# The second tile's first slices on other PSUM banks, five of them begun early, and the last batch's v in the buffer of the q and k rows

## The chip, the cores and the metric

The kernel runs on one core of one Trainium2 chip, in one launch. The metric is the device time of an execution in microseconds (us); the median of three runs is given. Engines are called as in the profile: PE (TensorE, matrix products), DVE (VectorE), ACT (ScalarE), POOL (GpSimd, which here also issues most loads) and SP (SyncE, which issues transposing DMAs and stores). PSUM has eight banks; each holds one 128 x 512 result in f32.

## The reference, cut to what matters

```python
def _attn_ref(q, k, v):                    # q, k, v: (8, 8, 576, 64) f32
    scores = scale * np.matmul(q, k.transpose(0, 1, 3, 2))
    rel = pos[:, None] - pos[None, :]
    mask = (rel >= 0) & (rel < 64)         # each row sees itself and the 63 rows before it
    ...                                    # softmax over the masked scores
    return np.matmul(attn, v)

def _moe_ref(x, w_in, w_out):              # x: (4608, 512), w_in: (512, 2048), w_out: (2048, 512)
    h = x @ w_in
    g = h * np.cos(h)
    return g @ w_out
```

The output of the attention, with the heads side by side, is x of the second part: 8 batches x 576 rows = 4608 rows of 512.

## The kernel before

**The tiles.** The 4608 rows are nine tiles (mt 0 to 8) of 512 rows. For a tile PE makes 16 slices of h (`first`, L347): slice ff is a 128 x 512 result summed over four k-steps `ks`, one for each pair of heads. ACT takes sin(h + pi/2) of a slice (L495), DVE multiplies it by h (gT, L498), and PE then makes four 128-row blocks of the output from the 16 gT slices (out_ps, L510), 64 products of 128 x 512. Copies of out_ps into out_sb go by DVE or ACT (`copy`, L108), and SP stores them.

**The attention of the next tiles runs between these products.** In units of 64 rows and one pair of heads: scores s_ps on PE (`burst`, L257), minimum and mask on DVE (`g_max`, L273), exp on ACT (`g_exp`, L284), reciprocal on DVE (L291), normalised weights w on POOL (`g_norm`, L298). w is transposed into wT by a DMA that SP issues (L310), or by PE through tw_ps and a copy (L307, L108). `values` (L326) multiplies v by wT into o_ps for one pair of heads; `put_x` casts o_ps into xT, the input of that tile's h. So k-step ks of a tile needs `put_x` of pair ks.

**The order** is written out by hand. `plan` holds steps with a time in slots (32 slots to a tile, one slot about 1 us); `pump(t)` issues all steps that are due at t. Every engine works through its own instructions in that order.

**The start of a tile.** The first SKEW = 3 slices are not made one after the other: `skewed` issues k-step ks of slices 0, 1 and 2 as soon as xT of pair ks is due, and the other slices follow whole. Tile 0 begins with other steps. In tile 1 (mt 1) `values` of pairs 0 and 1 stand between the last output products of tile 0, then come k-step 0 of three slices, then `values` of pairs 2 and 3, then the rest.

**The banks.** Five banks have names (X0, X1, S, O0, O1); the pool `t` has three more. Scores of tile 0's stage use X1, S and X0 (`S_BANKS`). Output products always use O0 and O1. The slices of h take the banks of a table in turn, `H_FIRST` for tile 0 and `H_BANKS` for all others:

```python
H_BANKS = ("X0", "O0", "X1", "S", "O1") * 2 + ("X0", "X1", "S", "O0", "O1", "t")
```

At the end of tile 0 the copy that empties O0 is put off by one line alone: `at(Q + 13.97, copy, "d", o_sb[:, e], o_ps[e])`, so it stands on DVE behind `put_x` of pairs 0 and 1.

**The rows and v.** q and k of batch b land in `rows(b)` (rowtiles[0] for all but batch 1, rowtiles[1] for batch 1); `turn` (L152) issues two transposing DMAs from there into T, which `burst` reads. v of batch b lands in `vtiles[b % 3]` (`load_v`, L158, five loads issued by POOL), and `spread_v` makes the shifted copies in the same buffer, on DVE for batches 2 to 7. Batch 7 has the last rows, so nothing more is loaded into rowtiles[0] after its two `turn` steps.

Of the kernel before, what the change touches and what calls it, by code (L numbers as in the profile page):

```python
# [31 lines left out]
PAIRS = 4  # L32
# [3 lines left out]
SKEW = 3  # L36
# [15 lines left out]
def kernel(  # L52
# [10 lines left out]
    B, H, S, D = q.shape  # L63
    assert (B, H, S, D) == (8, 8, 576, 64)
    scale = 1.0 / math.sqrt(D)
    d_model = H * D
# [13 lines left out]
    rowtiles = [const.tile([128, 2 * PAIRS * S], BF16, name=f"rows{i}") for i in range(2)]  # L80
    vtiles = [const.tile([128, NU - 1, d_model], BF16, name=f"v{i}") for i in range(3)]
# [10 lines left out]
    st = {}  # L92

    H_FIRST = ("O1", "X0", "X1", "S", "O0") * 3 + ("X0",)
    H_BANKS = ("X0", "O0", "X1", "S", "O1") * 2 + ("X0", "X1", "S", "O0", "O1", "t")
    S_BANKS = ("X1", "S", "X0")
    BURSTS = (("X0", "X1", "S", "t"), ("X0", "X1", "S", "t", "t", "t"))
# [2 lines left out]
    def bank(which, name):  # L102
        if which == "t":
            return ps_t.tile([128, 512], F32, tag="t", name=name)
        return ps.tile([128, 512], F32, tag=which, name=name)

    def copy(engine, out, in_):
        {"a": nc.scalar.copy, "p": nc.gpsimd.tensor_copy}.get(engine, nc.vector.tensor_copy)(out, in_)  # L108
# [22 lines left out]
    def rows(b):  # L131
        return rowtiles[1 if b == 1 else 0]
# [18 lines left out]
    def turn(b, lo, hi):  # L151
        nc.sync.dma_start(out=turned(b)[:, lo * 512:hi * 512].rearrange("d (g x) -> d g x", x=128),  # L152
                          in_=rows(b)[:, lo * 512:hi * 512], transpose=True)

    def load_v(b, c):
        n = 128 if c < 4 else 64
        vt = vtiles[b % 3][:n, 2 * c if c < 4 else 2 * c - 1]
        nc.gpsimd.dma_start(out=vt.rearrange("p (h d) -> p h d", h=H),  # L158
                            in_=v[b, :, c * 128:c * 128 + n, :].rearrange("h p d -> p h d"))


    def spread_v(b, half, engine="p"):
        vt = vtiles[b % 3]
        to, of = ((vt[0:64, 1:7:2], vt[0:64, 2:8:2]), (vt[64:128, 1:8:2], vt[64:128, 0:7:2]))[half]
        if engine == "dma":
            nc.sync.dma_start(out=to, in_=of)
        else:
            copy(engine, to, of)
# [150 lines left out]
    def values(mt, p):  # L319
        st["o", mt, p] = o_ps = bank("S", "o_ps") if mt > 1 and p == PAIRS - 1 else ps_t.tile([128, MT], F32, tag="t", name="o_ps")  # L320
        for i in range(TU):
            b, j = divmod(mt * TU + i, NU)
            wT = st["wT", (b, p, j)]
            cross = st["cross", (b, p, j)]
            for h in range(2):
                nc.tensor.matmul(out=o_ps[64 * h:64 * h + 64, 64 * i:64 * i + 64],  # L326
                                 lhsT=vtiles[b % 3][:, max(j - 1, 0), 128 * p + 64 * h:128 * p + 64 * h + 64],
                                 rhs=wT[:, 64 * (h ^ cross):64 * (h ^ cross) + 64], start=True, stop=True, skip_group_check=True)


# [7 lines left out]
    def exp_table():  # L338
        nc.scalar.activation(small, small, AF.Exp, scale=0.0)
# [3 lines left out]

    def first(mt, ff, ks, start, stop):
        if start:
            st["h", ff] = bank((H_BANKS if mt else H_FIRST)[ff], "h_ps")
        nc.tensor.matmul(out=st["h", ff], lhsT=w_in_sb[:, ks, ff * 128:ff * 128 + 128],  # L347
                         rhs=st["xT", mt][:, ks], start=start, stop=stop)

    def skewed(mt, ks, n):  # L350
        for ff in range(SKEW):
            first(mt, ff, ks, n == 0, n == PAIRS - 1)

    def last_rows(gT, o_sb):
        ms = MT // 128 - 1
        for which, lo, hi in (("O1", 0, LAST), ("S", LAST, d_model)):
            o_ps = bank(which, "out_ps")[:, lo:hi]
            for ff in range(n_ff):
                nc.tensor.matmul(out=o_ps, lhsT=gT[ff // 2][:, ff % 2, ms * 128:ms * 128 + 128],  # L359
                                 rhs=w_out_sb[:, ff, lo:hi], start=ff == 0, stop=ff == n_ff - 1)  # L360
            to = moe.tile([128, MT], F32, tag="sin", name="last_sb", bufs=4)[:, lo:hi] if lo else o_sb[:, 1, lo:hi]
            copy("d" if lo else "a", to, o_ps)
            (nc.sync if lo else nc.scalar).dma_start(out=out[n_mt * MT - 128:n_mt * MT, lo:hi], in_=to)

    def store(o_sb, mt, ms0, e, n):
        r0 = mt * MT + (ms0 + e) * 128
        nc.sync.dma_start(out=out[r0:r0 + n * 128].rearrange("(a p) f -> p a f", p=128), in_=o_sb[:, e:e + n])
# [3 lines left out]
    def at(time, fn, *args):  # L371
        plan.append((time, len(plan), fn, args))

    def pump(time):
        plan.sort(key=lambda x: x[:2])
        while plan and plan[0][0] <= time:
            _, _, fn, args = plan.pop(0)
            fn(*args)
# [3 lines left out]
    n = n_first  # L382
    for t in range(B - 1):
        last = max(i for i, units in enumerate(groups) if units[0][0] == t + 1)
        time = T * t + Q - 1.4
# [9 lines left out]
        for i in range(last + 1 - n):  # L395
            time = times[i] + (0.3 if i > 3 and t else 0)
# [30 lines left out]
    for half in range(2):  # L427
        at(17.5, spread_v, 1, half, "dma")
    for mt in range(1, n_mt):
        for p in range(PAIRS):  # L430
            time = max(ready[b, p - p % 2 + i // TU, j] for i in range(2 * TU) for b, j in (divmod(mt * TU + i % TU, NU),))
            time = max(time, 25.5) if mt == 1 else T * mt - (8.01 if mt == n_mt - 1 else 1.01)
            at(time, values, mt, p)
            if mt == 1:
                at(time + 0.3 + 0.2 * (p % 2), put_x, mt, p)
            else:
                at(time + 0.2 + 0.1 * p, put_x, mt, p, "a" if p == 1 else None)

# [10 lines left out]
    for c in range(4):  # L449
        load_v(0, c)  # L450
# [25 lines left out]
    for mt in range(n_mt):  # L476
        base = mt * T
        gT = []
        if mt:
            for ks in range(PAIRS):  # L480
                pump(max([base - 1] + [time for time, _, fn, args in plan
                                       if fn is put_x and args[:2] == (mt, ks)
                                       or mt == 1 and fn is values and args == (mt, ks + 1)]))
                skewed(mt, ks, ks)
        for ff in range(n_ff):
            for ks in range(PAIRS):
                if ff >= SKEW:
                    first(mt, ff, ks, ks == 0, ks == PAIRS - 1)
            h_ps = st.pop(("h", ff))
            sin = moe.tile([128, MT], F32, tag="sin", name="sin", bufs=4)  # L490
            if ff % 2 == 0:
                gt = moe.tile([128, 2, MT], BF16, tag="gT", name="gT", bufs=n_ff // 2 + 2)
                gT.append(gt)
            e = ff % 2
            nc.scalar.activation(sin, h_ps, AF.Sin, bias=math.pi / 2.0)  # L495
            if ff == n_ff - 1 and mt < B - 1:
                exp_table()
            nc.vector.tensor_tensor(out=gt[:, e], in0=h_ps, in1=sin, op=ALU.mult)  # L498
            pump(base + ff)
        half = n_ff // 2 if mt == 0 else n_ff  # L500
        for ms0 in range(0, MT // 128, 2):
            o_sb = moe.tile([128, 2, d_model], F32, tag="out", name="out_sb", bufs=3)
            o_ps = [bank(which, "out_ps") for which in (("O0",) if mt == n_mt - 1 and ms0 else ("O0", "O1"))]
            for step, (lo, e) in enumerate([(lo, e) for lo in range(0, n_ff, half) for e in range(2)]):
                ms = ms0 + e
                if mt == n_mt - 1 and ms == MT // 128 - 1:
                    last_rows(gT, o_sb)
                    break
                for ff in range(lo, lo + half):
                    nc.tensor.matmul(out=o_ps[e], lhsT=gT[ff // 2][:, ff % 2, ms * 128:ms * 128 + 128],  # L510
                                     rhs=w_out_sb[:, ff], start=ff == 0, stop=ff == n_ff - 1)
                    if ff % 4 == 3:
                        if ff == n_ff - 1:
                            if mt or not ms0 or e:
                                copy("a" if e else "d", o_sb[:, e], o_ps[e])
                            else:
                                at(Q + 13.97, copy, "d", o_sb[:, e], o_ps[e])
                            if mt == n_mt - 1:
                                store(o_sb, mt, ms0, e, 1)
                        pump(base + Q + 4 * ms0 + step * half // 4 + ff % half // 4)  # L520
            if mt < n_mt - 1:
                at(base + T + (1.5 if mt else 3) + ms0 / 2, store, o_sb, mt, ms0, 0, 2)
# [30 lines left out]
```

## Time and profile before

| | before |
|---|---|
| time, median of 3 runs | 309.13 us (307.98 to 309.42) |
| the profiled execution's own time | 308.6 us |
| its span in the profile | 306.8 us |
| granted PE clock, mean | 0.994 |
| busy share PE, ACT, DVE, POOL | 96%, 77%, 72%, 56% |
| tile 1, its first h product to its last (PE timeline) | 60.19 to 75.70 us |
| a later tile (mt 3), first h product to the next tile's | 123.57 to 154.40 us |

The span runs from the first to the last instruction that the profiler saw; 308.6 - 306.8 = 1.8 us lie around it. A row of the timeline has the start, the duration, engine, line, operation and operands, a count, and in brackets the engine's idle time before it with what ended it. The end of a PE row is modelled; the starts are what is measured, so distances between starts are used here.

### The profile page before, as it was taken

How to read it: one execution, taken by the hardware profiler on the slowest of the kernel's cores; microseconds unless marked ns; L12 is line 12 of the kernel's file. 1: busy time of each engine (PE TensorE's matmuls, PEld its weight loads, DVE VectorE, ACT ScalarE, POOL GpSimd, SP SyncE). 2: the span in 40 equal slices, each digit the busy share in tenths (PEclk: the TensorE clock that was granted, in tenths of full speed). 3: DMA queues.
4: the chain of work that ended last, by engine and by line, in shares of the span. 5: the costliest groups of instructions: out<-in, count | busy, mean ns of one | idle time of the engine just before them, and what ended most of it. 6: DMA issues, size and time to landing. Idle time of an engine off the chain costs nothing.

```text
span 306.8 us, 7883 instructions
## 1 busy us (share of the span) xinstructions
PE 294.2 (96%) x2668; PEld 143.0 (47%) x2668; DVE 219.9 (72%) x833; ACT 235.2 (77%) x785; POOL 171.8 (56%) x200
## 2 busy tenths in 40 slices
PE   3979999999999999999999999999999999999995
PEld 2645444444444444544454445444544454454443
DVE  2896889777787778787877887788778877236701
ACT  4798689867998799869986998699869986116600
POOL 8997247897565976597649766957803630000000
PEclk9989999999999999999999999999999999999999
DMA  6999999699999999999999999999994441011011
GB/s 87 170 210 207 208 165 154 95 157 144 227 135 166 180 198 130 169 166 209 138 169 180 200 134 171 161 214 119 139 167 151 88 138 54 0 72 69 0 71 68
DMA packets 165577, 43.58 MB, mean 142 GB/s; under 512 B 154720, under 2 KB 161056, under 8 KB 165536
## 3 DMA queue, kind: packets, MB, share of 16 engines
q0 software_dynamic: 99632, 18.36, 76.5%
q1 hardware_dynamic: 65760, 24.52, 41.8%
q8 instruction: 21, 0.34, 0.4%
q10 hardware_dynamic: 144, 0.20, 0.2%
q14 instruction: 20, 0.16, 0.2%
HBM read 36.70 MB, written 9.44 MB: 150 GB/s over the span
## 4 chain that ended last, share of the span: by engine, by line
PE 87%; DVE 6%; ACT 2%; DMA 1%; POOL 1%; issue 1%; POOLq 0%; DVEq 0%
PE h_ps L347 41%; PE out_ps L510 36%; PE s_ps L257 3%; PE o_ps L326 3%; DMA rows<-in_k_dram 1%; PE out_ps L359 1%; DVE s L273 1%; DVE negm L269 1%; DVE w L298 1%; DVE v L108 1%; PE tk_ps L182 1%; DVE wT L108 1%; DVE out_sb L108 1%; POOL rows L141 1%; PE s_ps L240 1%
## 5 line engine op out<-in xcount | busy, mean ns | idle before, releaser
L347 PE MATMUL h_ps<-xT,w_in 128*128 128x512 bf16 x576 | 128.2, 380 | 1.5 <-DVE out_sb L108 0.6
L510 PE MATMUL out_ps<-w_out,gT 128*128 128x512 bf16 x560 | 125.1, 379 | 0.2 <-DVE gT L498 0.2
L498 DVE TENSOR_TENSOR gT<-h_ps,sin 128x512 bf16<-128x512 f32 x144 | 95.6, 688 | 35.8 <-ACT sin L495 35.6
L495 ACT ACTIVATE sin<-h_ps 128x512 f32<-128x512 f32 x144 | 83.1, 599 | 34.7 <-PE h_ps L347 33.8
L284 ACT ACTIVATE e<-s,negm 128x128 f32<-128x128 f32 x256 | 98.7, 389 | 0.3 <-DVE negm L273 0.3
L298 POOL TENSOR_TENSOR w<-e,rden 128x512 bf16<-128x512 f32 (+1 forms) x76 | 74.4, 993 | 36.4 <-DVE rden L291 34.4
L347 PEld LDWEIGHTS <-w_in 128*128 128x128 bf16 x576 | 55.8, 98 | 67.6 <-issue 2.9
L510 PEld LDWEIGHTS <-gT 128*128 128x128 bf16 x560 | 53.2, 98 | 62.4 <-issue 0.2
L273 DVE CUSTOM_DVE_ANT_0 s<-s_ps,mask 128x128 f32<-128x128 f32 x256 | 58.0, 284 | 0.5 <-PE s_ps L257 0.5
L284 ACT ACTIVATION_READ_ACCUMULATOR e<-s,negm 128x1 f32 x256 | 48.6, 190 | 0.0
L158 POOL DMA_DIRECT2D v<-in_v_dram x40 | 34.0, 882 | 11.9 <-DMA rows<-in_k_dram 6.8
L148 POOL DMA_DIRECT2D rows<-in_q_dram x30 | 25.4, 864 | 24.1 <-DMA T<-rows 14.2
L108 ACT COPY out_sb<-out_ps 128x512 f32<-128x512 f32 (+1 forms) x18 | 10.2, 566 | 24.9 <-PE out_ps L510 19.5
L148 POOL DMA_DIRECT2D rows<-in_k_dram x30 | 25.5, 894 | 2.8 <-DMA T<-rows 2.3
L291 DVE RECIPROCAL rden<-den 128x4 f32<-128x4 f32 (+1 forms) x80 | 13.7, 172 | 18.3 <-ACT e L284 17.5
L108 DVE CAST xT<-o_ps 128x512 bf16<-128x512 f32 x27 | 17.5, 679 | 6.3 <-PE o_ps L326 6.0
L273 DVE DVE_READ_ACCUMULATOR2_ANT negm<- 128x1 f32 x256 | 21.2, 83 | 0.0
L108 DVE COPY out_sb<-out_ps 128x512 f32<-128x512 f32 x18 | 12.4, 688 | 12.1 <-PE out_ps L510 12.1
L326 PEld LDWEIGHTS <-v 128*64 128x64 bf16 x576 | 10.8, 114 | 4.7 <-issue 2.5
L326 PE MATMUL o_ps<-wT,v 128*64 128x64 bf16 x576 | 12.7, 199 | 0.1
L284 ACT ACTIVATE e<-s_ps,negm 128x128 f32<-128x128 f32 x32 | 11.4, 393 | 1.6 <-DVE negm L269 1.4
L257 PE MATMUL s_ps<-T 64*64 64x128 bf16 x512 | 12.1, 221 | 0.0
(50 smaller groups left out, 137.1 us busy)
## 6 DMA issues: line engine op xcount, KB each, us to landing
out_dram<-out_sb SPq DMA_DIRECT2D x16, 512.0 KB, 6.0
v<-in_v_dram POOLq DMA_DIRECT2D x32, 128.0 KB, 8.6
rows<-in_q_dram POOLq DMA_DIRECT2D x24, 128.0 KB, 5.6
rows<-in_k_dram POOLq DMA_DIRECT2D x24, 128.0 KB, 8.8
w_out<-in_moe_w_out_dram POOLq DMA_DIRECT2D x2, 1024.0 KB, 16.8
w_in<-in_moe_w_in_dram POOLq DMA_DIRECT2D x2, 768.0 KB, 12.5
wT<-w SPq DMA_TRANSPOSE x66, 4.0
out_dram<-out_sb SPq DMA_DIRECT2D x3, 256.0 KB, 2.0
```

The source lines that it names most:

```text
L108: {"a": nc.scalar.copy, "p": nc.gpsimd.tensor_copy}.get(engine, nc.vector.tensor_copy)(out, in_)
L148: nc.gpsimd.dma_start(out=rows(b)[lo:lo + n, slot * 512:slot * 512 + 512].rearrange("p (h d) -> p h d", h=H), in_={"q": q, "k": k}[name][b ...
L158: nc.gpsimd.dma_start(out=vt.rearrange("p (h d) -> p h d", h=H), in_=v[b, :, c * 128:c * 128 + n, :].rearrange("h p d -> p h d"))
L257: nc.tensor.matmul(out=s_ps[cross][to, u].rearrange("p (a t) -> p a t", a=2), lhsT=q_cols(b, p, j)[d], rhs=k_cols(b, p, j)[d], start=True, ...
L273: nc.vector.tensor_tensor_reduce(out=s[:, u], in0=s_ps[:, u], in1=mask[:, 2 - j % 2 if j else 0], scale=-scale if b else -1.0, scalar=BIG, ...
L284: nc.scalar.activation(e[:, u], s[:, u], AF.Exp, bias=negm[:, u:u + 1], scale=1.0 if n < n_first else -1.0, accum_out=den[:, u:u + 1])
L298: (nc.gpsimd if engine == "p" else nc.vector).tensor_tensor(out=w[:, 0:u], in0=e[:, 0:u], op=ALU.mult, in1=rden[:, 0:u].unsqueeze(2).to_br ...
L326: nc.tensor.matmul(out=o_ps[64 * h:64 * h + 64, 64 * i:64 * i + 64], lhsT=vtiles[b % 3][:, max(j - 1, 0), 128 * p + 64 * h:128 * p + 64 * ...
L347: nc.tensor.matmul(out=st["h", ff], lhsT=w_in_sb[:, ks, ff * 128:ff * 128 + 128], rhs=st["xT", mt][:, ks], start=start, stop=stop)
L495: nc.scalar.activation(sin, h_ps, AF.Sin, bias=math.pi / 2.0)
L498: nc.vector.tensor_tensor(out=gt[:, e], in0=h_ps, in1=sin, op=ALU.mult)
L510: nc.tensor.matmul(out=o_ps[e], lhsT=gT[ff // 2][:, ff % 2, ms * 128:ms * 128 + 128], rhs=w_out_sb[:, ff], start=ff == 0, stop=ff == n_ff - 1)
```

## The change

```diff
     H_FIRST = ("O1", "X0", "X1", "S", "O0") * 3 + ("X0",)
+    H_SECOND = ("X0", "X1", "S", "O0", "O1") * 3 + ("t",)
...
+    def values_of(b):
+        return rowtiles[0][:, 0:8 * d_model].rearrange("p (s x) -> p s x", s=8) if b == B - 1 else vtiles[b % 3]
+
     def load_v(b, c):
         n = 128 if c < 4 else 64
-        vt = vtiles[b % 3][:n, 2 * c if c < 4 else 2 * c - 1]
+        vt = values_of(b)[:n, 2 * c if c < 4 else 2 * c - 1]
...
     def spread_v(b, half, engine="p"):
-        vt = vtiles[b % 3]
+        vt = values_of(b)
...
-                                 lhsT=vtiles[b % 3][:, max(j - 1, 0), 128 * p + 64 * h:128 * p + 64 * h + 64],
+                                 lhsT=values_of(b)[:, max(j - 1, 0), 128 * p + 64 * h:128 * p + 64 * h + 64],
...
-            st["h", ff] = bank((H_BANKS if mt else H_FIRST)[ff], "h_ps")
+            st["h", ff] = bank((H_FIRST, H_SECOND, H_BANKS)[min(mt, 2)][ff], "h_ps")
...
+    def skew(mt):
+        return 5 if mt == 1 else SKEW
+
     def skewed(mt, ks, n):
-        for ff in range(SKEW):
+        for ff in range(skew(mt)):
             first(mt, ff, ks, n == 0, n == PAIRS - 1)
...
             if mt == 1:
-                at(time + 0.3 + 0.2 * (p % 2), put_x, mt, p)
+                at(time + 0.3 + 0.2 * (p % 2), put_x, mt, p, "a" if p == 1 else None)
...
-                skewed(mt, ks, ks)
+                if mt > 1 or ks < 2:
+                    skewed(mt, ks, ks)
+            if mt == 1:
+                for ff in range(skew(1)):
+                    for ks in range(2, PAIRS):
+                        first(1, ff, ks, False, ks == PAIRS - 1)
         for ff in range(n_ff):
             for ks in range(PAIRS):
-                if ff >= SKEW:
+                if ff >= skew(mt):
                     first(mt, ff, ks, ks == 0, ks == PAIRS - 1)
```

It does two separate things. **In tile 1** the slices take their banks from a new table: slices 0 to 2 use X0, X1 and S, slices 3 and 4 use O0 and O1. Five slices instead of three get their k-steps 0 and 1 early, and k-steps 2 and 3 of these five then come slice by slice. The cast of pair 1 (`put_x`) goes to ACT instead of DVE. **For batch 7** v is loaded into the first 4096 columns of rowtiles[0], spread there and read from there.

On PE, at the start of tile 1, before. The rows begin behind the last output product of tile 0; h_ps_1331, 1333 and 1335 are slices 0, 1 and 2 in banks X0, O0 and X1, and o_ps_1339 is `values` of pair 2:

```order
L347 LDWEIGHTS w_in_77
L347 MATMUL h_ps_1331<-xT_1312,w_in_77 128x512
L347 LDWEIGHTS w_in_77
L347 MATMUL h_ps_1333<-xT_1312,w_in_77 128x512
L347 LDWEIGHTS w_in_77
L347 MATMUL h_ps_1335<-xT_1312,w_in_77 128x512
L326 LDWEIGHTS v0_74
L326 MATMUL o_ps_1339<-wT_1022,v0_74 64x64
```

The same place after; h_ps_1331 to 1339 are slices 0 to 4 in banks X0, X1, S, O0 and O1, and o_ps_1343 is `values` of pair 2:

```order
L351 LDWEIGHTS w_in_77
L351 MATMUL h_ps_1331<-xT_1312,w_in_77 128x512
L351 LDWEIGHTS w_in_77
L351 MATMUL h_ps_1333<-xT_1312,w_in_77 128x512
L351 LDWEIGHTS w_in_77
L351 MATMUL h_ps_1335<-xT_1312,w_in_77 128x512
L351 LDWEIGHTS w_in_77
L351 MATMUL h_ps_1337<-xT_1312,w_in_77 128x512
L351 LDWEIGHTS w_in_77
L351 MATMUL h_ps_1339<-xT_1312,w_in_77 128x512
L330 LDWEIGHTS v0_74
L330 MATMUL o_ps_1343<-wT_1022,v0_74 64x64
```

The product into O0 moved from second to fourth place, one into O1 now stands fifth, and both stand ahead of `values` of pair 2.

On DVE, the same stretch before (xT is `put_x`, wT the copy from tw_ps, out_sb the copy that empties O0):

```order
L291 RECIPROCAL rden<-den 128x4
L108 CAST xT<-o_ps 128x512 x2
L108 COPY wT<-tw_ps 128x384
L108 COPY out_sb<-out_ps 128x512
L291 RECIPROCAL rden<-den 128x4
L108 CAST xT<-o_ps 128x512 x2
```

And after:

```order
L295 RECIPROCAL rden<-den 128x4
L109 CAST xT<-o_ps 128x512
L109 COPY wT<-tw_ps 128x384
L109 COPY out_sb<-out_ps 128x512
L295 RECIPROCAL rden<-den 128x4
L109 CAST xT<-o_ps 128x512 x2
```

One cast of the first two has left DVE; on ACT it stands between the 20 exps and the copy that empties O1. The five loads of v of batch 7 keep their place on POOL, but before they waited for PE's reads of batch 4's v, and after the first waits for the first half of batch 7's `turn` to land and the fourth for its second half. The first DVE copy of `spread_v` for batch 7 waited for three semaphores and now waits for eleven, the added ones of older DMAs into and out of rowtiles[0].

## The prediction

> **What bounds the kernel now.** I read the shares of the page first, then the chain of work that ended last, then PE's waits, and last the timeline around the start of tile 1, engine by engine.
>
> ```profile
> PE 294.2 (96%) x2668; PEld 143.0 (47%) x2668; DVE 219.9 (72%) x833; ACT 235.2 (77%) x785; POOL 171.8 (56%) x200
> ...
> PE 87%; DVE 6%; ACT 2%; DMA 1%; POOL 1%; issue 1%; POOLq 0%; DVEq 0%
> ```
>
> ```profile
> PE tq_ps L182 <- DMA rows<-in_q_dram: 4.8, 1, 4.8
> PE h_ps L347 <- DVE out_sb L108: 0.6, 1, 0.6
> ```
>
> PE is busy 96% of the span and carries 87% of the last chain, so a microsecond that PE loses in the middle is a microsecond of the time, and work of other engines counts only where PE waits for it. The second fence has two of PE's waits (us in total, times, longest). The longest is in the start-up and is not touched. The other, one wait of an h product for a copy into out_sb, is where the change sets in. PE's timeline places it, and the last row, of the chain, shows what follows:
>
> ```profile
> 60.19 0.38 PE L347 MATMUL h_ps<-xT,w_in 128*128 128x512 bf16 x1
> 61.22 0.59 PE L347 MATMUL h_ps<-xT,w_in 128*128 128x512 bf16 x2 [0.65 <-DVE out_sb L108]
> 61.74 0.70 PE L326 MATMUL o_ps<-wT,v 128*64 128x64 bf16 x32
> 62.36 3.84 PE L347 MATMUL h_ps<-xT,w_in 128*128 128x512 bf16 x17
> ```
>
> ```profile
> 62.43 13.27 PE h_ps L347 x61
> ```
>
> Slice 0 starts at 60.19, slice 1 (bank O0) only at 61.22. Seventeen products one behind the other take 3.84 us; without the 0.38 of the last that is 16 steps of 0.216 us. So slice 1 could have started at 60.19 + 0.216 = 60.41, and PE lost 61.22 - 60.41 = 0.81 us. From 62.43 on PE runs through to the tile's last slice without a wait. The engines that PE meets here:
>
> ```profile
> 57.33 0.29 DVE L273 CUSTOM_DVE_ANT_0 s<-s_ps,mask 128x128 f32<-128x128 f32 x1
> ...
> 59.01 1.29 DVE L108 CAST xT<-o_ps 128x512 bf16<-128x512 f32 x2 [0.66 <-PE o_ps L326]
> 60.22 0.35 DVE L108 COPY wT<-tw_ps 128x384 bf16<-128x384 bf16 x1
> 60.48 0.68 DVE L108 COPY out_sb<-out_ps 128x512 f32<-128x512 f32 x1
> ...
> 62.23 1.29 DVE L108 CAST xT<-o_ps 128x512 bf16<-128x512 f32 x2 [0.98 <-PE o_ps L326]
> ```
>
> ```profile
> 59.14 0.39 ACT L284 ACTIVATE e<-s,negm 128x128 f32<-128x128 f32 x1
> 60.39 0.58 ACT L108 COPY out_sb<-out_ps 128x512 f32<-128x512 f32 x1 [0.77 <-PE out_ps L510]
> 92.55 0.59 ACT L108 CAST xT<-o_ps 128x512 bf16<-128x512 f32 x1
> ```
>
> The copy that empties O0 stands on DVE behind two casts and a small copy and ends at 60.48 + 0.68 = 61.16; PE starts 0.06 us later.
>
> **The change, part by part: tile 1.** *O0.* DVE has one cast fewer ahead of the copy. Two casts held DVE from 59.01 to the next row's start, 60.22, about 0.60 each. The wT copy then starts at about 59.62, the O0 copy at 59.88, and O0 is free at 59.88 + 0.68 + 0.06 = 60.62. Slices 0, 1 and 2 start at 60.19, 60.41 and 60.62: their banks X0, X1 and S last held scores, which DVE finished reading at 57.33 + 0.29 = 57.62. Slice 3 on O0 is due at 60.84, 0.22 after the bank is free. *O1.* Slice 4 is due at 60.19 + 4 x 0.216 = 61.05. ACT empties O1 from 60.39, when PE's last out_ps is done, to 60.97; with 0.06 O1 is free at 61.03, a cover of 0.02 us only. Ahead of that copy ACT now casts pair 1. It is free at 59.14 + 0.39 = 59.53 and a cast takes 0.59 (last row, the same cast in the next tile), so it is done near 60.15, and the copy starts at 60.39 as before. Were the cast later by x, PE would lose x - 0.24 at slice 4.
>
> The cast costs ACT nothing, since it stood idle 0.77 us there, and what is behind the copy keeps its time. *`values` of pairs 2 and 3* started 0.09 behind their due time (61.74 against 61.22 + 2 x 0.216 = 61.65). I keep that: 60.19 + 5 x 0.216 + 0.09 = 61.36, with two more products already done. *Casts of pairs 2 and 3.* DVE began them 62.23 - 61.74 = 0.49 after `values`; now at 61.85, both done at 63.14. `values` held PE for 62.36 - 61.74 = 0.62, so k-step 1 of five slices runs from 61.98, slice 0's k-step 2 starts at 63.06 and its k-step 3 at 63.28, 0.14 after the cast of pair 3 (0.08 with the 0.06 of a release). Before, 62.36 + 6 x 0.216 = 63.66 stood against 62.23 + 1.29 = 63.52, the same cover.
>
> ```profile
> L498 DVE TENSOR_TENSOR gT<-h_ps,sin 128x512 bf16<-128x512 f32 x144 | 95.6, 688 | 35.8 <-ACT sin L495 35.6
> L495 ACT ACTIVATE sin<-h_ps 128x512 f32<-128x512 f32 x144 | 83.1, 599 | 34.7 <-PE h_ps L347 33.8
> ```
>
> *Sine and gT.* Slice 0 is whole at 63.28 + 0.38 = 63.66; a sin of 0.60 and a gT of 0.69 later X0 is free, near 65.0. Slice 5 wants it at 63.06 + 10 x 0.216 = 65.22. The last six slices have the same banks in both tables, so the scores and output products behind them meet nothing new.
>
> Term: **-0.81 us**. Bounds: -0.90 if the 0.09 goes too; -0.4 if the covers at O1 and pair 3 fail by 0.2 us each.
>
> **Is it kept to the end?** The work of ACT and DVE in the later stages starts from PE's products, so it moves with PE. Loads hang on POOL's queue and may not. The nearest deadline is T of batch 2, which the first scores in tile 1's stage read:
>
> ```profile
> L257 PEld LDWEIGHTS <-T x32: 102/107/107, 75.6 to 76.0; 64*64 64x64 bf16 x32
> ...
> L152 SPq DMA_TRANSPOSE T<-rows x2: 1510/2692/3873, 58.4 to 65.3; - x2
> ...
> DMA to landing us min/median/max: 8.2/8.3/8.4
> ```
>
> The second half lands by 65.3 + 8.4 = 73.7; the scores, at 75.6 before, now come at 74.8. The cover shrinks from 1.9 to 1.1 us and holds.
>
> **Batch 7's v.** Sums and copies are the same; what changes is when the loads may start, and the waits at the first spread copy. The rows: T of batch 7 with the scores that read it, v's loads, what stands behind them on POOL, and DVE and PE where v is used.
>
> ```profile
> L257 PEld LDWEIGHTS <-T x32: 103/107/107, 229.9 to 230.3; 64*64 64x64 bf16 x32
> L152 SPq DMA_TRANSPOSE T<-rows x2: 3060/3655/4250, 215.0 to 218.3; - x2
> DMA to landing us min/median/max: 7.1/8.8/10.6
> L158 POOL DMA_DIRECT2D v<-in_v_dram x5: 725/893/938, 217.1 to 220.7; - x5
> DMA to landing us min/median/max: 5.8/9.0/9.2
> 234.03 1.03 POOL L298 TENSOR_TENSOR w<-e,rden 128x512 bf16<-128x512 f32 x1 [12.64 <-DVE rden L291]
> 244.01 0.92 DVE L108 COPY v<-v 64x1536 bf16<-64x1536 bf16 x1
> 245.91 0.69 DVE L108 CAST xT<-o_ps 128x512 bf16<-128x512 f32 x1
> 246.66 0.81 PE h_ps L347 x3
> L152 SPq EVENT_SEMAPHORE  x35: 17/28/28, 58.0 to 218.2; - x35
> ```
>
> T's halves land at 215.0 + 7.1 = 222.1 and 218.3 + 10.6 = 228.9. The v loads ran from 217.1. Now the first waits until 222.1 and the fourth until 228.9; the fifth is issued near 229.8 and POOL is free at 230.5. Behind them stands w at 234.03, 3.5 us later. The last v lands at 229.8 + 9.2 = 239.0; the spread wants it at 244.01. That cover of 5 us makes the cost 0. The eight added waits on DVE are for DMAs long done, and the old copy's three show no idle ahead of it. SP's semaphore instructions take 28 ns (last row), so they are bounded by 8 x 0.028 = 0.22; I take 0. It matters, since the cast of 245.91 stands behind that copy, ends at 246.60, and releases tile 7's first h at 246.66. A gain is possible too: T's second half took 10.6 us with v's loads beside it and landed only 1.0 us ahead of the scores at 229.9. Where it comes later, the change saves that wait; bound 0.5 us, the distance of the median from the profiled execution.
>
> **Sum.** 308.6 - 0.81 + 0 = 307.8 us for an execution like the profiled one. That one lies 0.53 under the median, so the median I forecast is 309.13 - 0.81 = **308.3 us**, 0.26% less. About 0.5%, 1.55 us, is what a measurement of this kernel can tell from no change; the three runs shown lie 1.44 us apart.
>
> **Rivals.** *Thin covers fail.* O1's copy and the cast of pair 3 come 0.2 us late each: half the gain, 308.7. For it: covers of 0.02 and 0.08. Against: both come from starts that the rows show, and the cover at pair 3 held before.
>
> *T of batch 2 becomes the wait.* It lands over 1.1 us later and takes the whole gain: 309.1. Against: both halves took 8.2 to 8.4 us.
>
> ```profile
> L158 POOL DMA_DIRECT2D v<-in_v_dram x40: 685/900/991, 6.4 to 220.7; - x40
> ...
> DMA to landing us min/median/max: 4.2/8.6/18.2
> ```
>
> *Slower: batch 7's v is late.* The fifth load, issued at 229.8, decides if it takes over 14.2 us to land, since the spread stands ready at 244.0. The slowest of v's 40 loads took 18.2. Then it lands at 248.0, DVE stands 4.0 us, and the cast and tile 7's first h with it: 308.3 + 4.0 = 312.3. For it: the load now runs beside the wT transposes and stores of that stage. Against: 9.2 us at most for these five.
>
> *Slower too: POOL's issues stretch beside DVE's work.* At five times the median of 0.90, 4.5 us each, the first three would hold POOL from 222.1 to 235.6, the fifth would be issued at 240.1 and land at 249.3, 5.3 us late: 313.6. Against: 40 issues took 685 to 991 ns, with DVE busy 72% of the span. The Trainium skill, "SBUF — State Buffer", section "Who interferes with whom", states the rule behind this: a DMA issued by GpSimd starves of descriptors while DVE holds a port pair that both share. No issue of this trace shows it.
>
> *More: the median run waits for T of batch 7.* Then 0.5 us more go: 307.8.
>
> **How the numbers follow.** Forecast 0.62, thin covers 0.14, T of batch 2 0.07, late v 0.06, stretched issues 0.01, wait for T of batch 7 0.10. The runs reach 1.15 below and 0.29 above their median. From the forecast that is 307.15 at the low end, 307.0 with the last case in it; at the high end it is 309.1 + 0.29 = 309.4, with T of batch 2 in it. Outside stay late v, stretched issues and the scatter's tails. Faster by over 0.5% means under 307.6: 0.10 from the forecast's scatter and 0.05 from the last case, 0.15. Slower: 0.07 from the two cases of batch 7 and 0.02 from scatter, 0.09. The rest, 0.76, is within 0.5%.
>
> **What would show it.** Right: PE's wait for out_sb is gone, five h products start 0.22 us apart, `values` of pair 2 starts 1.2 us after the first of them, every later tile starts 0.8 us earlier, and v of batch 7 is issued in two groups behind T. Wrong: a new wait of h for ACT's out_sb or a cast, of the scores for T, or of tile 7's first cast for the spread.

## The result, and the profile after

| | before | after |
|---|---|---|
| median | 308.72 us (18 runs, 307.98 to 309.54) | 308.01 us (18 runs, 307.33 to 308.38) |
| ratio to before, 95% interval | | 0.9974 (0.9964 to 0.9983) |
| the profiled execution's own time, its span | 308.6, 306.8 us | 308.04, 306.0 us |
| slice 0 of tile 1, start (PE timeline) | 60.19 us | 60.33 us |
| from there to tile 1's first scores (D) | 15.44 us | 14.64 us |
| from there to the last output products | 239.67 us | 238.95 us |

Before was run again beside after, hence its 18 runs and a median of 308.72. After is 0.71 us faster by the medians, and 0.26% by the ratio. The interval leaves out 1, so the effect is real, though it is half of the 0.5% that the prediction called visible. The two rows that end D, tile 1's first scores in before and then in after:

```profile
75.63 0.64 PE L257 MATMUL s_ps<-T 64*64 64x128 bf16 x32
```

```profile
74.97 0.64 PE L261 MATMUL s_ps<-T 64*64 64x128 bf16 x32
```

The page of after, the shares of busy time and the chain that ended last:

```profile
PE 294.1 (96%) x2668; PEld 143.1 (47%) x2668; DVE 219.3 (72%) x832; ACT 235.6 (77%) x786; POOL 171.9 (56%) x200
...
PE 83%; ACT 5%; DVE 5%; DMA 3%; POOL 1%; issue 1%; POOLq 0%; DVEq 0%
```

DVE has one instruction fewer and ACT one more: the cast that moved. PE still carries the chain. Its waits in after (us in total, times, longest):

```profile
PE tq_ps L186 <- DMA rows<-in_q_dram: 5.1, 2, 4.8
PE tw_ps L311 <- POOL w L302: 1.9, 3, 1.5
PE h_ps L351 <- ACT xT L109: 0.5, 1, 0.5
PE h_ps L351 <- DVE xT L109: 0.2, 1, 0.2
```

The wait of h for out_sb is gone, and no wait has its place: those of h for xT are the same 0.5 and 0.2 us, in the start-up, that before has. The start of tile 1 on PE:

```profile
60.33 1.24 PE L351 MATMUL h_ps<-xT,w_in 128*128 128x512 bf16 x5
61.51 0.69 PE L330 MATMUL o_ps<-wT,v 128*64 128x64 bf16 x32
62.13 4.06 PE L351 MATMUL h_ps<-xT,w_in 128*128 128x512 bf16 x18
```

Five products stand in one row, without a gap, and `values` of pair 2 follows 61.51 - 60.33 = 1.18 us behind the first. The same stretch on DVE and on ACT:

```profile
59.16 0.69 DVE L109 CAST xT<-o_ps 128x512 bf16<-128x512 f32 x1 [0.65 <-PE o_ps L330]
59.77 0.35 DVE L109 COPY wT<-tw_ps 128x384 bf16<-128x384 bf16 x1
60.03 0.68 DVE L109 COPY out_sb<-out_ps 128x512 f32<-128x512 f32 x1
```

```profile
59.67 0.57 ACT L109 CAST xT<-o_ps 128x512 bf16<-128x512 f32 x1
60.53 0.58 ACT L109 COPY out_sb<-out_ps 128x512 f32<-128x512 f32 x1 [0.29 <-PE out_ps L522]
```

O0 is empty at 60.03 + 0.68 = 60.71, and with the 0.06 of a release slice 3, due at 60.33 + 3 x 0.216 = 60.98, has 0.21 us of cover. O1 is empty at 61.11, with the release 61.17, and slice 4 is due at 61.19: 0.02 us.

For batch 7, T's two transposing DMAs, then v's five loads with POOL's row for them, and DVE's two spread copies with the cast behind. The last fence has the semaphore instructions ahead of the first copy:

```profile
L153 SPq DMA_TRANSPOSE T<-rows x2: 1835/2450/3064, 214.8 to 218.0; - x2
DMA to landing us min/median/max: 4.6/4.8/5.1
```

```profile
L162 POOL DMA_DIRECT2D rows<-in_v_dram x5: 705/887/938, 220.4 to 224.0; - x5
DMA to landing us min/median/max: 3.9/5.1/5.6
220.42 4.29 POOL L162 DMA_DIRECT2D rows<-in_v_dram  x5 [3.80 <-DMA T<-rows]
243.45 0.92 DVE L109 COPY rows<-rows 64x1536 bf16<-64x1536 bf16 x1
244.48 0.69 DVE L109 COPY rows<-rows 64x2048 bf16<-64x2048 bf16 x1
245.35 0.69 DVE L109 CAST xT<-o_ps 128x512 bf16<-128x512 f32 x1
```

```profile
L109 DVEq EVENT_SEMAPHORE  x5: 49/50/50, 242.9 to 243.3; - x5
```

The loads do wait for T (3.80 us of idle on POOL), run as one group and have landed by 224.0 + 5.6 = 229.6, 13.8 us before the first copy. The eleven waits at that copy cost nothing that the trace shows. Most of them are taken up by five semaphore instructions of 0.05 us (one in before) that stand ahead of the copy, and these run while DVE is still at its masks: the copy starts 0.21 us after the last mask has begun in both kernels (243.45 - 243.24 and 244.01 - 243.80), without idle time. From the copy to the cast it is 1.90 us, as before (244.01 to 245.91).

### The profile page after: what moved, and what is told of

It reads as the page before. It is cut to its first block, busy times and chain, and to the rows that moved or that the text cites. A ratio compares the mean times of both kernels' runs of the same rounds, so it can differ in the third digit from the quotient of the medians.

```text
span 306.0 us, 7884 instructions
## 1 busy us (share of the span) xinstructions
PE 294.1 (96%) x2668; PEld 143.1 (47%) x2668; DVE 219.3 (72%) x832; ACT 235.6 (77%) x786; POOL 171.9 (56%) x200
## 4 chain that ended last, share of the span: by engine, by line
PE 83%; ACT 5%; DVE 5%; DMA 3%; POOL 1%; issue 1%; POOLq 0%; DVEq 0%
PE h_ps L351 41%; PE out_ps L522 33%; ACT e L288 3%; PE o_ps L330 3%; PE s_ps L261 3%; DMA rows<-in_q_dram 1%; PE out_ps L366 1%; DVE s L277 1%; DMA wT<-w 1%; DVE negm L273 1%; DVE w L302 1%; ACT L343 1%; PE tk_ps L186 1%; PE tq_ps L186 1%; POOL w L302 1%
## 5 line engine op out<-in xcount | busy, mean ns | idle before, releaser
L162 POOL DMA_DIRECT2D v<-in_v_dram x35 | 29.6, 869 | 12.4 <-DMA rows<-in_k_dram 5.8
L295 DVE RECIPROCAL rden<-den 128x4 f32<-128x4 f32 (+1 forms) x80 | 13.8, 172 | 18.3 <-ACT e L288 17.1
L261 PEld LDWEIGHTS <-T 64*64 64x64 bf16 x512 | 8.2, 106 | 8.3 <-DVE negm L277 3.9
L330 PEld LDWEIGHTS <-v 128*64 128x64 bf16 x504 | 9.7, 114 | 4.4 <-issue 2.3
```

The lines of the kernel that those rows point to most:

```text
L261: nc.tensor.matmul(out=s_ps[cross][to, u].rearrange("p (a t) -> p a t", a=2), lhsT=q_cols(b, p, j)[d], rhs=k_cols(b, p, j)[d], start=True, ...
```

## The experiments

Two theories were to be told apart from the start: that the 0.8 us comes from the banks alone (first slices on banks that the scores left free long ago), or from the five slices and the moved cast (more work ahead of `values`). Beside that, the part on batch 7 was to be priced by itself. In the table D is the distance from slice 0 to tile 1's first scores, G from there to tile 2's first h, R from there to tile 8's first h. The start-up is left out of all three. Each is read from one profiled execution of a kernel; the medians are of 7 to 12 runs, but for the 18 of before and after.

| kernel | D | G | R | median, us | ratio, 95% interval |
|---|---|---|---|---|---|
| before | 15.44 | 17.06 | 182.99 | 308.72 | |
| after | 14.64 | 17.18 | 182.96 | 308.01 | 0.9974 (0.9964 to 0.9983) |
| tile 1 alone | 14.64 | 17.15 | 183.01 | 308.2 | 0.9973 (0.9959 to 0.9988) |
| batch 7's v alone | 15.45 | 17.11 | 183.24 | 309.28 | 1.001 (0.9995 to 1.0025) |
| bank table alone | 14.64 | 17.15 | 182.98 | 308.2 | 0.9977 (0.9962 to 0.9992) |
| five slices, old banks | 14.85 | 17.08 | 183.00 | 308.52 | 0.9991 (0.9975 to 1.0007) |
| O0 first | see there | 17.16 | 182.99 | 309.04 | 1.0007 (0.9995 to 1.0019) |
| five slices, cast on DVE | 15.02 | 17.07 | 182.99 | 308.44 | 0.9989 (0.9974 to 1.0004) |
| T of batch 3 later | 14.63 | 17.00 | 182.99 | 307.8 | 0.9974 (0.9963 to 0.9985) |
| spread of v earlier | 14.64 | 16.75 | 185.38 | 309.49 | 1.0026 (1.0012 to 1.004) |
| banks and T of batch 3 | 14.64 | 17.04 | 183.14 | 307.83 | 0.9967 (0.9956 to 0.9979) |
| all T later | 14.64 | 17.00 | 184.53 | 308.62 | 0.9999 (0.9983 to 1.0016) |

Each ratio is to the runs of before on the same chip, whose medians were 308.72 to 308.85.

**Each part alone.** First after with v of batch 7 back in its old buffer, then before with only that part:

```diff
-        return rowtiles[0][:, 0:8 * d_model].rearrange("p (s x) -> p s x", s=8) if b == B - 1 else vtiles[b % 3]
+        return vtiles[b % 3]
```

> The tile 1 part of the change alone; v of batch 7 stays in its own buffer. D is the distance on PE from the first h product of tile 1 to the first scores of its stage: 15.44 us in before (60.19 to 75.63), 14.64 in the changed kernel (60.33 to 74.97). Theory (all of the gain comes from tile 1): D 14.64, ratio to before 0.997 to 0.998, and T of batch 7 lands late again, its second half about 10 us after its issue. Rival (v's place takes a wait for T of batch 7 out of the typical run): D 14.64, but only about 0.3 us faster than before, ratio 0.999.

```diff
+    def values_of(b):
+        return rowtiles[0][:, 0:8 * d_model].rearrange("p (s x) -> p s x", s=8) if b == B - 1 else vtiles[b % 3]
...
-        vt = vtiles[b % 3][:n, 2 * c if c < 4 else 2 * c - 1]
+        vt = values_of(b)[:n, 2 * c if c < 4 else 2 * c - 1]
```

> The batch 7 part alone: v in the buffer of the q and k rows, tile 1 as before. Theory: no change, ratio 0.9995 to 1.0005, D 15.44, although T of batch 7 lands about 6 us earlier, since the scores never waited for it. Rival (the typical run waited for T): ratio 0.9985 (0.5 us). Rival on the slower side (the added waits on DVE or late loads): ratio above 1.0005 and a gap ahead of the first cast of tile 7.

Tile 1 alone brings what after brings: D 14.64, ratio 0.9973. The part on batch 7 changes D by 0.01 and has a ratio whose interval reaches from 0.05% faster to 0.25% slower: no gain in it, and no cost that can be told from none. Its 1.001 lies above the 0.9995 to 1.0005 that was expected, within the noise, and the gap ahead of tile 7's first cast that the slower rival asked for isn't there: from the first copy to the cast it is 1.90 us again. Its R is 0.25 longer in the profile, but at tile 2's end, far ahead of batch 7's v, and after, which has the same edit, shows 182.96. T of batch 7 with v's loads beside it, in tile 1 alone:

```profile
L153 SPq DMA_TRANSPOSE T<-rows x2: 3049/3516/3984, 213.2 to 216.4; - x2
DMA to landing us min/median/max: 5.0/6.6/8.3
```

It landed late again, 8.3 us where about 10 were expected. With batch 7's v alone it takes 5.1, as in after.

**The bank table alone**: three slices and all casts as before.

```diff
+    H_SECOND = ("X0", "X1", "S", "O0", "O1") * 3 + ("t",)
...
-            st["h", ff] = bank((H_BANKS if mt else H_FIRST)[ff], "h_ps")
+            st["h", ff] = bank((H_FIRST, H_SECOND, H_BANKS)[min(mt, 2)][ff], "h_ps")
```

> Only the bank table of tile 1 is changed (X0, X1, S, O0, O1); three slices begun as before, all casts on DVE, v as before. Theory (the loss was the bank O0 at second place and nothing else): the first three products 0.22 us apart, D 14.63, ratio 0.997 to 0.998, the same as the whole change. Rival (the five slices and the cast on ACT are needed): with three slices the casts of pairs 2 and 3 come too late for k-steps 2 and 3, PE waits 0.3 to 0.4 us there, D about 15.0, ratio 0.9987.

D is 14.64 here too. PE's timeline at the start of tile 1:

```profile
60.55 0.81 PE L348 MATMUL h_ps<-xT,w_in 128*128 128x512 bf16 x2
61.30 0.69 PE L327 MATMUL o_ps<-wT,v 128*64 128x64 bf16 x32
...
75.19 0.64 PE L258 MATMUL s_ps<-T 64*64 64x128 bf16 x32
```

(Of its three first products the trace holds two.) With three slices on X0, X1 and S, `values` follows 0.75 us behind slice 0, and O0 is not asked for until they are over. So the table is the whole gain, and the five slices and the cast add nothing to it.

**Five slices and the cast on ACT, but the old banks** (X0, O0, X1, S, O1), v as before:

```diff
+        return 5 if mt == 1 else SKEW
...
+                at(time + 0.3 + 0.2 * (p % 2), put_x, mt, p, "a" if p == 1 else None)
```

> Five slices, k-steps 2 and 3 slice by slice and the cast on ACT, but with the old bank table (X0, O0, X1, S, O1); v as before. Theory: O0 is asked for at the second place, 0.22 us after the first product, and is free 0.43 us after it, since DVE has one cast less ahead of the copy: a wait of 0.21, D 14.85, ratio about 0.998. Rival (the order of the banks is all): the wait stays 0.81, D 15.44, ratio 1.000. Rival (the five slices alone hide it): D 14.64.

```profile
59.38 0.68 DVE L109 COPY out_sb<-out_ps 128x512 f32<-128x512 f32 x1
59.69 1.46 PE L351 MATMUL h_ps<-xT,w_in 128*128 128x512 bf16 x4
74.54 0.64 PE L261 MATMUL s_ps<-T 64*64 64x128 bf16 x32
```

Slice 0 starts at 59.69, O0 is free at 59.38 + 0.68 + 0.06 = 60.12. The second product, on O0, was due at 59.91, so 0.21 us of the wait are left, and D is 74.54 - 59.69 = 14.85, 0.21 over 14.64. So 0.59 of the 0.80 us come here with the old banks. By the rows it is the cast's move that gains them, since O0 is free 60.12 - 59.69 = 0.43 behind slice 0 instead of 61.22 - 60.19 = 1.03; the cast without the five slices was not run. The ratio, 0.9991 against an expected 0.998, is not told from 1 by itself.

**Five slices and the new banks, but pair 1's cast left on DVE**, v as before:

```diff
-                at(time + 0.3 + 0.2 * (p % 2), put_x, mt, p, "a" if p == 1 else None)
+                at(time + 0.3 + 0.2 * (p % 2), put_x, mt, p)
```

> The tile 1 part with new banks and five slices, but the cast of pair 1 stays on DVE ahead of the copy that empties O0; v as before. D is the distance from the first h product of tile 1 to its stage's first scores, 14.64 in the changed kernel. Theory: O0 is free 1.03 us after the first product as in before, slice 3 asks for it at 0.65, a wait of 0.38, D 15.02, ratio about 0.9985; so the cast on ACT is needed because five slices are begun. Rival (the cast's place doesn't matter): D 14.64.

```profile
60.34 0.81 PE L351 MATMUL h_ps<-xT,w_in 128*128 128x512 bf16 x2
61.37 0.59 PE L351 MATMUL h_ps<-xT,w_in 128*128 128x512 bf16 x2 [0.22 <-DVE out_sb L109]
61.89 0.69 PE L330 MATMUL o_ps<-wT,v 128*64 128x64 bf16 x32
...
75.36 0.64 PE L261 MATMUL s_ps<-T 64*64 64x128 bf16 x32
```

Slice 3 was due at 60.34 + 0.65 = 60.99 and starts at 61.37, when DVE has emptied O0: 0.38 lost, and D is 75.36 - 60.34 = 15.02. So in the change the cast on ACT is needed only because five slices ask for O0 ahead of `values`; with three slices neither is.

**O0 first**: before, with the worst order of banks for tile 1.

```diff
+    H_SECOND = ("O0", "X0", "X1", "S", "O1") * 3 + ("t",)
```

> The kernel before with O0 moved to the first place in tile 1's bank table (O0, X0, X1, S, O1); nothing else. E is the distance on PE from the first of the last four out_ps products of tile 0 to the first scores of tile 1's stage: 16.31 us in before (59.32 to 75.63), 15.50 in the changed kernel. Theory (PE stands until the copy empties O0, whatever is behind it): the first h product itself waits, 1.03 us instead of 0.81, E 16.53, about 0.2 us slower than before, ratio 1.0007. Rival (a fixed price of such a wait, whatever its place): E 16.31.

```profile
59.70 1.03 PE L511 MATMUL out_ps<-w_out,gT 128*128 128x512 bf16 x4
61.60 0.81 PE L348 MATMUL h_ps<-xT,w_in 128*128 128x512 bf16 x2 [0.87 <-DVE out_sb L109]
...
76.23 0.64 PE L258 MATMUL s_ps<-T 64*64 64x128 bf16 x32
```

Here slice 0 itself waits, so the distance E is taken instead, from the last four output products of tile 0 to tile 1's first scores: 76.23 - 59.70 = 16.53, against 75.63 - 59.32 = 16.31 before. Slice 0 was due 0.87 behind these four, as before (60.19 - 59.32), so at 60.57. The wait grows from 0.81 to 1.03 us: the end of the copy decides, and the same wait costs one more slot of 0.216 when the product that asks for O0 stands one place earlier.

**Where G comes from.** G is 0.12 us longer in after than in before. Two ends of it were tried in after: T of batch 3 issued later, so that it doesn't run beside the last wT transposes, and the spread copies of v put earlier on DVE.

```diff
-        at(t0 - (3.1 if b == 2 else 5.6), turn, b, 0, 5)
-        at(t0 - (3 if b == 2 else 5.5), turn, b, 5, 9)
+        at(t0 + (0.65 if b == 3 else -3.1 if b == 2 else -5.6), turn, b, 0, 5)
+        at(t0 + (0.66 if b == 3 else -3 if b == 2 else -5.5), turn, b, 5, 9)
```

> The changed kernel with the two transposing DMAs of batch 3's rows issued one wT transpose later. At the start of tile 2 the changed kernel's PE waits about 0.27 us for the sixth wT transpose, which takes 3.3 us to land with those two DMAs right behind it; that wait was 0.15 us in before. Theory (they share the DMA engines): it lands in about 2.3 us, the wait goes, the 64 o_ps products of tile 2 take 1.45 instead of 1.73 us, tile 2's h starts 0.2 to 0.3 us earlier against the first scores of tile 1's stage (17.18 us from there in the changed kernel, 17.06 in before). Rival (POOL's loads are what slows it): no change, 17.18.

```diff
-            at(t0 + 27.5 + half, spread_v, b, half, "d")
+            at(t0 + 25.9 + 0.6 * half, spread_v, b, half, "d")
```

> The changed kernel with DVE's spread copies of v for batches 2 to 7 about 1.6 to 2 slots earlier, ahead of the last six mask steps of the stage. In the changed kernel PE waits at the start of tiles 2 to 5 for the second spread copy, 0.21, 0.18, 0.15 and 0.12 us. Theory: these waits go and the time falls by about 0.6 us under the changed kernel, ratio to before 0.9955. Rival (the first cast or the wT transposes, late by then too, take over): the waits change their name and the ratio stays at 0.9974.

With T later G is 17.00, 0.18 under after; 0.2 to 0.3 was expected. The wT transpose that PE waits for still takes 3.09 us to land, against 3.27 in after, 3.16 in before and the 2.3 expected, so T beside it accounts for 0.18 us of that time; what makes up the rest stays open. The ratio is the same as after's. But the 0.12 is hardly the price of the change: G is 17.16 with O0 first, where the scores come later than before, and 17.07 and 17.08 in two kernels where they come earlier. G follows the landing of that wT transpose, which takes 3.09 to 3.27 us in the eleven kernels other than the earlier spread, and after has the 3.27. That this is chance and no part of the change is likely, but with one trace for each kernel it is not shown.

The earlier spread failed. It did what it was meant to for `values` (G 16.75), and lost more behind it. One of PE's waits and two rows of its timeline there:

```profile
PE h_ps L351 <- ACT xT L109: 1.2, 4, 0.3
```

```profile
92.16 0.81 PE L351 MATMUL h_ps<-xT,w_in 128*128 128x512 bf16 x2
93.24 13.32 PE L351 MATMUL h_ps<-xT,w_in 128*128 128x512 bf16 x60 [0.28 <-ACT xT L109]
```

DVE's rows of the same kernel, at the ends of tile 1 and of tile 3:

```profile
89.52 0.69 DVE L109 COPY v<-v 64x2048 bf16<-64x2048 bf16 x1
...
90.33 0.26 DVE L277 CUSTOM_DVE_ANT_0 s<-s_ps,mask 128x128 f32<-128x128 f32 x1
...
150.06 1.12 DVE L109 COPY v<-v 64x1536 bf16<-64x1536 bf16 x1 [0.55 <-DMA v<-in_v_dram]
```

The copies now stand ahead of DVE's last masks, ACT's exps wait for these, and ACT's cast of pair 1 stands behind the exps: what `values` gained, k-step 1 of h waits for (93.24, when the cast of pair 1 is done). At the end of tile 3 v had not landed when DVE reached the copy, DVE stood 0.55 us with the masks behind it, and over all later tiles R grew by 2.4 us.

**Two ways to a faster version.** The two edits that moved something, without the rest of the change (before, with the bank table and T of batch 3 later); and after with every later T put off in the same way:

```diff
-        at(t0 - (3.1 if b == 2 else 5.6), turn, b, 0, 5)
-        at(t0 - (3 if b == 2 else 5.5), turn, b, 5, 9)
+        at(t0 + (-3.1 if b == 2 else 0.65), turn, b, 0, 5)
+        at(t0 + (-3 if b == 2 else 0.66), turn, b, 5, 9)
```

> Before with two edits only: the bank table of tile 1's h (three slices begun early, all casts of pairs 0 and 1 on DVE, v of batch 7 in its old buffer), and the turn of batch 3 moved behind the start of tile 2's h, so that its transposes do not run beside the last wT transposes. Theory (the bank table is the whole gain of tile 1, and T of batch 3 beside the last wT transpose is what costs a few tenths at the end of tile 1): from slice 0 of tile 1 to the first scores 14.64 us, from these scores to tile 2's first h 17.00 instead of 17.06 in the profile of before, the gap ahead of the values of tile 2's last pair but one 0.12 us, ratio 0.9969. Rival (five slices and the cast on ACT matter in runs that were not profiled): the two distances as said, but a ratio of 0.9985 or more.

> After with the turns of batches 3 to 7 all moved 6.2 us later in the planner's time, so that one transposing DMA of wT more stands ahead of each T on SP's queue. Theory (the last transposes of wT land 0 to 0.3 us late at the ends of tiles 1 and 2, because T of the next batch runs beside them): from tile 1's first scores to tile 2's h 17.00 instead of 17.18 us, from tile 2's h to tile 3's 30.87 as in the profile of after but never over 30.9, the tiles behind as in after, ratio 0.9967. Rival (the wT transpose is not slowed by T but by its own late start behind w): 17.1 to 17.2, ratio 0.9974. Second rival (the rows of the next batch are loaded into the buffer that T empties, and land too late for their own turn): a new wait of scores for T and a ratio over 1.

The first has the best ratio of all, 0.9967, with D 14.64 as expected and G 17.04 against an expected 17.00; its interval holds after's 0.9974, so that it beats after is not shown, only that it is as good with two small edits. The second gave the whole gain back, 0.9999. G is 17.00 as the theory had it, but the ends of tiles 4 and 5 grew by 0.8 and 0.9 us. There, T later means that POOL issues the next rows and then v later (its last load of v at 174.69 instead of 172.48), and its products w run late and back to back. POOL, DVE and PE of this kernel, and then POOL and DVE of after, at the end of tile 4:

```profile
177.39 4.81 POOL L302 TENSOR_TENSOR w<-e,rden 128x512 bf16<-128x512 f32 x5
181.01 1.74 DVE L109 COPY v<-v 64x1536 bf16<-64x1536 bf16 x1
183.60 0.98 PE L330 MATMUL o_ps<-wT,v 128*64 128x64 bf16 x50 [0.77 <-DVE v L109]
174.69 0.69 POOL L162 DMA_DIRECT2D v<-in_v_dram  x1 [0.53 <-DMA rows<-in_k_dram]
```

```profile
172.48 0.69 POOL L162 DMA_DIRECT2D v<-in_v_dram  x1 [1.96 <-PE out_ps L522]
181.41 0.83 POOL L302 TENSOR_TENSOR w<-e,rden 128x384 bf16<-128x384 f32 x1 [0.33 <-DVE rden L295]
181.85 0.93 DVE L109 COPY v<-v 64x1536 bf16<-64x1536 bf16 x1
```

The spread copy takes 1.74 us instead of 0.93, and `values` waits for it. Counted from the tile's first h (153.00 with all T later, 153.85 in after) it starts at 28.0 us in both and ends 0.82 us later, which is what the end of tile 4 grew by.

## Why the prediction was right, point by point

- **The time.** Forecast were 308.3 us, and after took 308.01. The gap of 0.3 is in the base and not in the term: the three runs of before had a median of 309.13, eighteen have 308.72, and 308.72 - 0.81 = 307.91.
- **Tile 1, the term of -0.81.** D fell by 0.80. `values` of pair 2 came 1.18 us behind slice 0 (1.17 was worked out), and the covers at O0 and O1 were 0.21 and 0.02 (0.22 and 0.02). The thin cover at O1 held in the five profiled executions that have the whole tile 1 part: after, tile 1 alone, T of batch 3 later, spread of v earlier and all T later, with D at 14.63 or 14.64. The interval of the ratio leaves out that both covers fail in most runs (0.4 us, 0.9987), but not that one of them does by 0.2.
- **Kept to the end.** From slice 0 to the last output products it is 239.67 before and 238.95 after, 0.72 less, as the medians (0.71). "Every later tile starts 0.8 us earlier" is what the rows don't show: their starts moved by 0.54 to 0.57, because this execution's slice 0 came 0.14 later and G was 0.12 longer. Slice 0 stands ahead of what the change touches; for G see above.
- **T of batch 2.** Both halves land by 65.5 + 8.3 = 73.8 in after, the scores read them at 74.97; the cover of 1.2 us (1.1 worked out) held.

```profile
L153 SPq DMA_TRANSPOSE T<-rows x2: 1432/2734/4037, 58.5 to 65.5; - x2
DMA to landing us min/median/max: 6.7/7.5/8.3
```

- **Batch 7's v, the term of 0.** Right in its sum, wrong on the way. The step that failed took T's landing of before, 10.6 us, for the landing after. That was the price of running beside v's loads, and with these put behind T's first half, T lands in 5.1. So the loads came as one group instead of two, POOL was free at 224.7 instead of 230.5, and the cover at the spread was 13.8 us instead of 5. The two rivals on the slow side (v late, issues stretched) never came near, with issues of 705 to 938 ns. The rival on the fast side would need a wait of 0.5 us for T in the median run; the edit alone has a ratio of at least 0.9995, 0.15 us, so that is ruled out. The 0.5 us themselves were the distance of the profiled execution from a median of three runs; from the median of eighteen it is 0.1. The bound of 0.22 us for the added waits was taken from SP's semaphore instructions; DVE's own take longer, 0.05 us, and cost nothing because they run under the masks.
- **What the working didn't see** is which part of the change its term comes from. It took the cast on ACT, the five slices and the banks together, and its sum for O0 holds for the three together; the runs show that the table does it alone, that five slices bring the wait for O0 back (0.38 us) and that the cast takes it away again.

## What to carry to other kernels

At a stage's border, give the first products the banks whose readers finished longest ago, and leave those that are being emptied to the products that come last: a table of names gave 0.8 us here, the whole of the change, while moving the cast to another engine mended, with the new table, only what the five slices had broken, and with the old table left 0.21 us of the wait. Before trusting a landing time for a DMA that is to be moved, ask what ran beside it in the trace. And a step moved out of the way of one wait moves everything queued behind it: all T later shortened one wait and made another, by way of POOL and DVE, on PE.

## What the runs showed of the hardware that was not expected

- **A DVE copy and a POOL product hold each other up.** The first spread copy has fewer elements than the second, 64x1536 against 64x2048, and takes longer, 0.92 us against 0.69. In both pairs of rows at the end of tile 4 it ends about 0.54 us after POOL's w: 181.85 + 0.93 = 182.78 behind 181.41 + 0.83 = 182.24 in after, and 181.01 + 1.74 = 182.75 behind 177.39 + 4.81 = 182.20 with all T later. It thus seems to stand still until POOL is done and then to run in 0.54. The other way round, DVE's second copy and the w that starts inside it in after, and then the first copy with POOL's w starting inside it, where the spread came earlier:

```profile
182.88 0.69 DVE L109 COPY v<-v 64x2048 bf16<-64x2048 bf16 x1
182.93 1.33 POOL L302 TENSOR_TENSOR w<-e,rden 128x384 bf16<-128x384 f32 x1 [0.70 <-DVE rden L295]
```

```profile
87.58 0.68 DVE L109 COPY v<-v 64x1536 bf16<-64x1536 bf16 x1
87.78 1.12 POOL L302 TENSOR_TENSOR w<-e,rden 128x512 bf16<-128x512 f32 x1 [0.99 <-DVE rden L295]
```

Here the copies keep their time, 0.68 us for the first one, and the w of 128x384 takes 1.33 us instead of 0.83. The Trainium skill, "SBUF — State Buffer", section "Who interferes with whom", says that copies in a two-port mode and GpSimd lock each other out for whole instructions; the rows agree. The kernel with all T later is where it cost time. No run was made for it alone.
- **Transposing DMAs beside loads.** T of batch 7 takes 6.4 to 11.0 us at most in the seven kernels where v's loads run beside it, and 5.0 to 5.1 in the five where they wait for its first half. The later the loads begin, the less it takes: 10.6 us when they begin 2.1 us behind T's first issue (before), 8.3 at 2.8 (tile 1 alone), 6.4 at 3.2 (O0 first).
- **Where the scatter is.** Eleven of the kernels share their start-up up to slice 0 of tile 1, and it starts at 59.65 to 60.77 us in their profiled executions. R lies between 182.96 and 183.01 in eight kernels; in two more it is 0.15 and 0.25 us longer, all of it at tile 2's end, where PE waits for a wT transpose that took 3.27 and 3.08 us to land, and 2.42 in before. So most of the 1.4 us between runs comes ahead of tile 1, and distances within a trace told 0.2 us apart where medians of 7 to 12 runs couldn't.
